# The MLP pair in another order: three output steps behind the first product, two products of one bank together, no step at the end

## The chip, the core and the metric

The kernel runs on one NeuronCore of a Trainium2 chip. TensorE (PE) multiplies, with its weight loads (PEld) shown apart; VectorE (DVE), ScalarE (ACT) and GpSimd (POOL) do the rest; SyncE (SP) issues most DMAs. Products land in PSUM, which has banks of 512 fp32 values per partition. The metric is the device time of one execution in microseconds (us); lower is better.

## The reference, cut to what matters

Three parts follow each other: a Fourier mixing layer, an RWKV channel mix, and an MLP on all 12288 rows. The change lies in the MLP:

```python
def _moe2_ref(x, w_in, w_out):          # x: 12288 x 256
    h = x @ w_in                        # 256 x 2048
    sp = np.where(h > 20.0, h, np.log1p(np.exp(np.minimum(h, 20.0))))
    g = h * np.tanh(sp)                 # "mish"
    return (g @ w_out).astype(np.float32)   # 2048 x 256
```

## The kernel before, in words

The rows are cut into 24 blocks `t` of 512. For each block the 2048 hidden features are taken in 8 pairs, `P = 8 t + r`, each of 256 features by 512 rows. Block 0 is multiplied directly (`emit_h`). For blocks 1 to 23 (184 pairs) `emit_hS` multiplies the pair's 2x2 blocks (two halves of the inner dimension and two of the features, against two halves of the rows) with seven block products in place of eight. `A(i, j)` is a block of the weights, `S_(k)` a prepared sum or difference of such blocks (`WS`), and `xS` holds the seven matching blocks or sums of the rows, which VectorE prepares for the next block in six pieces (`make_xS`).

Every fp32 number is split into a high and a low part, so one product is three matmuls of 128x256 (`prod`, L1075). The accumulators are two PSUM banks a pair, `xy` and `z`, each with two halves of 256 columns, and two sets of them alternate between pairs. The seven products share partial sums: the first goes into `xy[0]`, ScalarE copies it to `z[0]` (L1085), further products are added on `xy` and `z`, ScalarE copies the whole bank `xy` to `ub` in SBUF (L1091), one more product is added on `xy[0]`, VectorE adds `xy[0]` and half of `ub` into `z[1]` (`add`, L1080), and after the last two products it adds the other half of `ub` into `xy[1]`. The mish of `z` is taken in the same pair (`mish`, L1057 and L1058: once into `gh`, once into `g`, with the difference `gl` on VectorE, L1061), and that of `xy` in the next pair, through `fin`.

The second matrix product runs three pairs behind (`LAG = 3`): `o(n)` takes n of the 8 output steps of pair `P - 3`. One step is two matmuls, `gh` by the high and low parts of `w_out` (512 columns, L1123) and `gl` by the high part (256 columns, L1124). Two steps (`m2` = 0, 1) belong to each of the four banks `o0` to `o3`, which are filled over the 8 pairs of a block. With the last pair of a block, `o_out` is called behind each second step: a ScalarE copy into `ob` (L1138), a VectorE sum (L1139) and a DMA out (L1140).

Each engine executes its own instructions in the order in which this code writes them, and waits by semaphores. No scheduler changes the order. A write to one half of a PSUM bank waits for a read of the other half.

Of the kernel before, what the change touches and what calls it, by code (L numbers as in the profile page):

```python
# [29 lines left out]
def kernel(  # L30
# [766 lines left out]
    def g_tiles(P):  # L797
        pool = w2p if P % 4 < 2 else pb
        return [pool.tile([128, 2, 512], F32R, tag=n, name=n, bufs=2) for n in ("gh", "gl")]
# [201 lines left out]
    def make_xS(t, k):  # L1001

        v = x2_t[t]
        o4 = last_order if t == NBLK - 1 else (lambda a, how=None: a)
        b11, b12, b21, b22 = (
            o4(v[:, j, 256 * h:256 * h + 256], "p (c n w) -> p c w n") for j in range(2) for h in range(2)
        )
        if k == 0:
            xT_t[0] = pb.tile([128, 4, 256], F32, tag="xT", name="xT", bufs=1)
            xS_t[t] = pb.tile([128, 2, 7, 256], F32R, tag="xS", name="xS", bufs=2)  # L1010
        xT, xS = xT_t[0], xS_t[t]

        def parts(l):
            if t == NBLK - 1:
                return [(o4(xS[:, l, i, :]), b) for i, b in enumerate((b11, b21, b22))]
            return [(xS[:, l, 0, :], b11), (xS[:, l, 1:3, :], v[:, 1, :].rearrange("p (h n) -> p h n", h=2))]

        def xt(o):
            return o4(xT[:, o, :])

        def sub(o, x0, x1):
            nc.vector.tensor_tensor(out=xt(o), in0=x0, in1=x1, op=ALU.subtract)

        if k == 0:
            sub(0, b12, b11)
            sub(2, b22, b12)
        elif k == 1:
            sub(1, b22, xt(0))
            sub(3, b21, xt(1))
        elif k == 2:  # L1030
            nc.vector.tensor_copy(out=xS[:, 0, 3:7, :], in_=xT)
        elif k == 3:
            nc.vector.tensor_tensor(out=xS[:, 1, 3:7, :], in0=xT, in1=xS[:, 0, 3:7, :], op=ALU.subtract)
        elif k == 4:
            for xs, b in parts(0):
                nc.vector.tensor_copy(out=xs, in_=b)
        else:
            for (xl, b), (xh, _) in zip(parts(1), parts(0)):
                nc.vector.tensor_tensor(out=xl, in0=b, in1=xh, op=ALU.subtract)
            x2_t.pop(t)  # L1040
# [11 lines left out]
    def mish(P, src, k):  # L1052

        gh, gl, g = g_t[P]
        ks = slice(0, 4, 3) if k == 0 else slice(1, 3)
        view = [v.rearrange("p m (h n) -> p (m h) n", h=2)[:, ks, :] for v in (gh, gl, g)]
        nc.scalar.activation(out=view[0], in_=src, func=AF.Mish)  # L1057
        nc.scalar.activation(out=view[2], in_=src, func=AF.Mish)  # L1058

        def low():  # L1060
            nc.vector.tensor_tensor(out=view[1], in0=view[2], in1=view[0], op=ALU.subtract)  # L1061

        return low

    def emit_hS(P, o):
        t, r = divmod(P, 8)
        xS = xS_t[t]
        f = [slice(256 * r + 128 * i, 256 * r + 128 * i + 128) for i in range(2)]
        xy, z = (psb.tile([128, 2, 256], F32, tag=f"h{k + P % 2}", name=n, bufs=1) for k, n in ((0, "xy"), (2, "z")))
        A = lambda i, j: (lambda l: WI[:, j, l, f[i]])  # L1070
        S_ = lambda k: (lambda l: WS[:, r, k, l, :])

        def prod(out, a, b, start=False):
            for n, (l, v) in enumerate(P3):
                nc.tensor.matmul(  # L1075
                    out=out, lhsT=a(l), rhs=xS[:, v, b, :], start=(start and n == 0), stop=False, skip_group_check=True
                )

        def add(out, x0, x1):
            nc.vector.tensor_tensor(out=out, in0=x0, in1=x1, op=ALU.add)  # L1080

        g_t[P] = g_tiles(P) + [pb.tile([128, 2, 512], F32, tag="g", name="g", bufs=2)]
        ub = pb.tile([128, 2, 256], F32, tag="ub", name="ub", bufs=2)
        prod(xy[:, 0, :], A(0, 0), 0, start=True)
        nc.scalar.copy(out=z[:, 0, :], in_=xy[:, 0, :])  # L1085
        low = fin[0]() if fin[0] else None
        prod(xy[:, 1, :], S_(2), 5)
        o(2)
        prod(xy[:, 0, :], S_(1), 4)
        prod(z[:, 0, :], A(0, 1), 1)  # L1090
        nc.scalar.copy(out=ub, in_=xy)  # L1091
        if low:
            low()
        if r > 1 and t + 1 < NBLK:
            make_xS(t + 1, r - 2)
        o(2)
        prod(xy[:, 0, :], S_(0), 3)
        add(z[:, 1, :], xy[:, 0, :], ub[:, 1, :])
        o(3)
        low = mish(P, z, 0)  # L1100
        prod(xy[:, 0, :], S_(3), 2)
        prod(xy[:, 1, :], A(1, 1), 6)
        add(xy[:, 1, :], xy[:, 1, :], ub[:, 0, :])
        low()
        o(1)
        fin[0] = lambda: mish(P, xy, 1)

    def new_o(t):
# [37 lines left out]
    for P in range(2, 8 * NBLK + LAG):  # L1146
        t, q = divmod(P, 8)
        steps = o_steps(P - LAG) if P >= LAG else iter(())

        def o(n):  # L1150
            for _ in range(n):
                next(steps, None)

        if P < 8 * NBLK:
            if q == 0 and 2 < t + 2 < NBLK:
                load_x2(t + 2)
            if t:
                if P == 8:
                    last_WS = make_WS(3, True)
                emit_hS(P, o)  # L1160
                if P < 12:
                    next(last_WS, None)
            else:
                emit_h(P)
                if q < 7:
                    make_xS(1, q - 2)
                if q == 6:
                    make_xS(1, 5)
                if q in (2, 4, 6):
                    for _ in make_WS(q // 2 - 1):  # L1170
                        pass
        elif fin[0]:
            fin[0]()()
            fin[0] = None
        o(9)
# [82 lines left out]
```

## Time and profile before

| what | value |
|---|---|
| median of 3 runs | 2101.61 us (2100.99 to 2104.11) |
| profiled execution, its own time | 2103.1 us |
| its span, from the first to the last instruction | 2101.3 us |
| TensorE busy | 1990.7 us (95% of the span) |
| weight loads busy | 1831.9 us (87%) |
| ScalarE busy | 1209.8 us (58%) |
| VectorE busy | 1127.0 us (54%) |
| mean granted TensorE clock | 0.997 |

Matmuls are pipelined: a row of the timeline shows 0.28 us for a matmul of 256 columns, while the next one starts before it ends. How long a matmul holds the engine is the distance between starts. A busy share is an average over the span, and the stage that the change touches is the last one, from about 966 us to the end.

### The profile page before, as it was taken

The numbers are of one execution on the slowest core, as the hardware profiler recorded it, in microseconds if no ns is written. First come the engines' busy times: TensorE is split into PE (matmuls) and PEld (weight loads), VectorE is DVE, ScalarE is ACT, GpSimd is POOL, SyncE is SP. The second block draws the span as 40 slices with busy tenths as digits, with TensorE's granted clock in tenths as the row PEclk, the third lists the DMA queues.
The fourth block names the chain that finished last, engine by engine and source line by source line (L and its number), as shares of the span: only waits on it lengthen the run. The fifth ranks groups of instructions, "written<-read, shape, count | busy, mean of one in ns | idle before, by whom it ended". The sixth has DMA issues, their size and how long they took to land.

```text
span 2101.3 us, 31779 instructions
## 1 busy us (share of the span) xinstructions
PE 1990.7 (95%) x12658; PEld 1831.9 (87%) x12658; DVE 1127.0 (54%) x1899; ACT 1209.8 (58%) x2151; POOL 130.7 (6%) x236
## 2 busy tenths in 40 slices
PE   7999999999999999999999999999999999999998
PEld 5888899999999999998888888888888888888887
DVE  3788765555555655446444444444544444444453
ACT  3666676666666666655555555555555555555554
POOL 1444410000000000000000000000000000000000
PEclk8999999999999999999999999999999999999999
DMA  9786422122121211110000010000000000000000
GB/s 282 217 243 205 149 78 68 57 63 67 56 67 54 69 54 59 41 43 21 21 21 21 21 29 23 21 21 21 26 26 21 21 21 21 21 21 31 11 11 21
DMA packets 71735, 122.93 MB, mean 58 GB/s; under 512 B 6370, under 2 KB 48580, under 8 KB 71588
## 3 DMA queue, kind: packets, MB, share of 16 engines
q1 hardware_dynamic: 68004, 108.33, 17.4%
q0 software_dynamic: 3584, 12.58, 1.6%
q8 instruction: 99, 1.62, 0.3%
q14 instruction: 48, 0.39, 0.1%
HBM read 70.56 MB, written 50.33 MB: 58 GB/s over the span
## 4 chain that ended last, share of the span: by engine, by line
PE 92%; ACT 4%; issue 1%; DVE 1%; DMA 1%; SPq 0%; ACTq 0%; DVEq 0%
PE xy L1075 21%; PE o L1123 17%; PE kp L686 13%; PE vp L871 13%; PE o L1124 8%; PE mxp L408 3%; ACT z L1085 3%; PE pp L825 3%; PE z L1075 3%; PE pp L509 2%; PE s1p L303 2%; PE s2p L352 2%; PE i1p L450 2%; PE k1p L408 2%; ACT ob L1138 0%
## 5 line engine op out<-in xcount | busy, mean ns | idle before, releaser
L1123 PE MATMUL o<-WO,gh 128*128 128x512 f32 x1536 | 574.0, 396 | 0.0
L1075 PE MATMUL xy<-xS,WS 128*128 128x256 f32 x2208 | 401.0, 290 | 95.0 <-ACT z L1085 94.1
L1075 PEld LDWEIGHTS xy<-xS,WS 128*128 128x128 f32 x2208 | 310.3, 188 | 162.8 <-ACT z L1085 131.7
L1124 PE MATMUL o<-WO,gl 128*128 128x256 f32 x1536 | 430.8, 280 | 0.0
L1061 DVE TENSOR_TENSOR gl<-g,gh 128x512 fp32r<-128x512 f32 x368 | 252.5, 686 | 172.4 <-ACT g L1058 172.4
L1123 PEld LDWEIGHTS o<-WO,gh 128*128 128x128 f32 x1536 | 288.8, 188 | 37.8
L686 PE MATMUL kp<-xk,WK 128*128 128x384 f32 x1524 | 291.9, 339 | 0.0
L1124 PEld LDWEIGHTS o<-WO,gl 128*128 128x128 f32 x1536 | 289.6, 189 | 0.2
L871 PE MATMUL vp<-kh,WV 128*128 128x384 f32 x1024 | 280.3, 335 | 0.0
L686 PEld LDWEIGHTS kp<-xk,WK 128*128 128x128 f32 x1524 | 264.1, 188 | 0.6 <-ACT yT L518 0.4
L858 DVE TENSOR_TENSOR kl<-kr,kh 128x768 fp32r<-128x768 f32 x128 | 123.0, 961 | 239.2 <-ACT kr L857 239.2
L1057 ACT ACTIVATE gh<-z 128x512 fp32r<-128x512 f32 x184 | 110.2, 599 | 217.7 <-DVE z L1080 217.7
L1080 DVE TENSOR_TENSOR xy<-xy,ub 128x256 f32<-128x256 f32 x184 | 79.6, 433 | 217.5 <-PE xy L1075 217.5
L1075 PE MATMUL xy<-xS,WI 128*128 128x256 f32 x1104 | 189.8, 280 | 0.0
L871 PEld LDWEIGHTS vp<-kh,WV 128*128 128x128 f32 x1024 | 186.7, 188 | 0.0
L1091 ACT COPY ub<-xy 128x512 f32<-128x512 f32 x184 | 108.2, 588 | 122.3 <-PE xy L1075 122.3
L871 PE MATMUL vp<-kl,WV 128*128 128x384 f32 x512 | 171.5, 335 | 0.0
L856 ACT ACTIVATE kh<-kr 128x768 fp32r<-128x768 f32 x128 | 108.2, 845 | 99.3 <-PE vp L871 99.3
L1075 PEld LDWEIGHTS xy<-xS,WI 128*128 128x128 f32 x1104 | 156.1, 188 | 7.9
L1080 DVE TENSOR_TENSOR z<-xy,ub 128x256 f32<-128x256 f32 x184 | 79.4, 432 | 152.4 <-PE xy L1075 131.9
L1085 ACT COPY z<-xy 128x256 f32<-128x256 f32 x184 | 65.8, 357 | 147.1 <-PE xy L1075 146.2
L849 ACT ACTIVATE kr<-kp 128x768 f32<-128x768 f32 x127 | 103.5, 815 | 74.4 <-PE kp L686 72.0
(150 smaller groups left out, 2818.2 us busy)
## 6 DMA issues: line engine op xcount, KB each, us to landing
scr<-Cs SPq DMA_DIRECT2D x48, 256.0 KB
D<-scr SPq DMA_DIRECT2D x32, 384.0 KB
x2d<-r POOLq DMA_DIRECT2D x32, 384.0 KB, 2.8
x<-x2d SPq DMA_DIRECT2D x24, 512.0 KB
out_dram<-ob SPq DMA_DIRECT2D x96, 128.0 KB
A<-scr SPq DMA_DIRECT2D x44, 256.0 KB
xs<-in_x_dram SPq DMA_DIRECT2D x24, 384.0 KB
scr<-xs SPq DMA_DIRECT2D x24, 384.0 KB
```

The lines of the kernel that those rows point to most:

```text
L686: nc.tensor.matmul(out=p, lhsT=WK[:, dh, w, f * 128:(f + 1) * 128], rhs=hl[:, v, dh, :], start=(i == 0), stop=(i == 5),)
L856: nc.scalar.activation(out=kh, in_=kr, func=AF.Square)
L858: nc.vector.tensor_tensor(out=kl, in0=kr, in1=kh, op=ALU.subtract)
L871: nc.tensor.matmul(out=p[:, o, 0:TA], lhsT=WV[:, f, w, o * 128:(o + 1) * 128], rhs=v[:, m, :], start=(f == 0 and i == 0), stop=(f == 7 and ...
L1057: nc.scalar.activation(out=view[0], in_=src, func=AF.Mish)
L1061: nc.vector.tensor_tensor(out=view[1], in0=view[2], in1=view[0], op=ALU.subtract)
L1075: nc.tensor.matmul(out=out, lhsT=a(l), rhs=xS[:, v, b, :], start=(start and n == 0), stop=False, skip_group_check=True)
L1080: nc.vector.tensor_tensor(out=out, in0=x0, in1=x1, op=ALU.add)
L1085: nc.scalar.copy(out=z[:, 0, :], in_=xy[:, 0, :])
L1091: nc.scalar.copy(out=ub, in_=xy)
L1123: nc.tensor.matmul(out=o[m], lhsT=gh[:, m2, ms], rhs=WO[:, f], start=(f == 0), stop=False)
L1124: nc.tensor.matmul(out=o[m][:, 0, :], lhsT=gl[:, m2, ms], rhs=WO[:, f, 0, :], start=False, stop=(f == 15))
```

## The change

In `emit_hS` the order of code lines changes, and nothing else. Before, the first product was followed by the product with `S_(2)` into `xy[1]`, two output steps, and the product with `S_(1)` into `xy[0]`. Now three output steps follow the first product, and then the products with `S_(1)` and `S_(2)` together. The output step that stood behind the last two products is gone from there; the pair still takes all 8 steps (3 + 2 + 3 in place of 2 + 2 + 3 + 1).

```diff
         prod(xy[:, 0, :], A(0, 0), 0, start=True)
         nc.scalar.copy(out=z[:, 0, :], in_=xy[:, 0, :])
         low = fin[0]() if fin[0] else None
+        o(3)
+        prod(xy[:, 0, :], S_(1), 4)
         prod(xy[:, 1, :], S_(2), 5)
-        o(2)
-        prod(xy[:, 0, :], S_(1), 4)
         prod(z[:, 0, :], A(0, 1), 1)
         nc.scalar.copy(out=ub, in_=xy)
...
         prod(xy[:, 1, :], A(1, 1), 6)
         add(xy[:, 1, :], xy[:, 1, :], ub[:, 0, :])
         low()
-        o(1)
         fin[0] = lambda: mish(P, xy, 1)
```

On TensorE, at the turn from one pair to the next, the kernel before has these rows: the last two products of a pair, the output step, the first product of the next pair (the fifth row), the product with `S_(2)`, two output steps, the product with `S_(1)`, the product into `z`.

```order
L1075 MATMUL xy<-xS,WS 128x256 x3
L1075 MATMUL xy<-xS,WI 128x256 x3
L1123 MATMUL o_15929<-WO,gh 128x512
L1124 MATMUL o_15929<-WO,gl 128x256
L1075 MATMUL xy<-xS,WI 128x256 x3
L1075 MATMUL xy<-xS,WS 128x256 x3
L1123 MATMUL o_15926<-WO,gh 128x512
L1124 MATMUL o_15926<-WO,gl 128x256
L1123 MATMUL o_15926<-WO,gh 128x512
L1124 MATMUL o_15926<-WO,gl 128x256
L1075 MATMUL xy<-xS,WS 128x256 x3
L1075 MATMUL z<-xS,WI 128x256 x3
```

The same place in the changed kernel, on TensorE, where the line numbers are one lower:

```order
L1075 MATMUL xy<-xS,WS 128x256 x3
L1075 MATMUL xy<-xS,WI 128x256 x6
L1122 MATMUL o_14558<-WO,gh 128x512
L1123 MATMUL o_14558<-WO,gl 128x256
L1122 MATMUL o_14558<-WO,gh 128x512
L1123 MATMUL o_14558<-WO,gl 128x256
L1122 MATMUL o_14559<-WO,gh 128x512
L1123 MATMUL o_14559<-WO,gl 128x256
L1075 MATMUL xy<-xS,WS 128x256 x6
L1075 MATMUL z<-xS,WI 128x256 x3
```

The last product of one pair and the first of the next now stand together (x6), three steps lie between the first product and the next one into the same bank, and the products with `S_(1)` and `S_(2)` stand together (x6) ahead of the one into `z`.

On VectorE, in the pair in which a block's output leaves, the kernel before has this order (`ob` are the output sums, `z` and `xy` the sums of L1080, `xT` a piece of the next block's operands):

```order
L1139 TENSOR_TENSOR ob<-ob,o_15471 128x256
L1061 TENSOR_TENSOR gl<-g,gh 128x512
L1022 TENSOR_TENSOR xT<-x_15279 128x256 x2
L1139 TENSOR_TENSOR ob<-ob,o_15472 128x256
L1080 TENSOR_TENSOR z<-xy,ub 128x256
L1139 TENSOR_TENSOR ob<-ob,o_15473 128x256
L1080 TENSOR_TENSOR xy<-xy,ub 128x256
L1061 TENSOR_TENSOR gl<-g,gh 128x2x256
L1139 TENSOR_TENSOR ob<-ob,o_15474 128x256
```

The changed kernel, on VectorE in the same pair:

```order
L1138 TENSOR_TENSOR ob<-ob,o_15468 128x256
L1061 TENSOR_TENSOR gl<-g,gh 128x512
L1022 TENSOR_TENSOR xT<-x_15279 128x256 x2
L1138 TENSOR_TENSOR ob<-ob,o_15469 128x256
L1080 TENSOR_TENSOR z<-xy,ub 128x256
L1138 TENSOR_TENSOR ob<-ob,o_15470 128x256
L1138 TENSOR_TENSOR ob<-ob,o_15471 128x256
L1080 TENSOR_TENSOR xy<-xy,ub 128x256
L1061 TENSOR_TENSOR gl<-g,gh 128x2x256
```

The fourth output sum moves ahead of the sum into `xy`; what stands ahead of the sum into `z` is as it was.

## Rows read from the trace of the kernel before

**Rows 1.** Windows: one stretch, busy time of each engine, granted clock.
```profile
core 0: us, PE busy (x) PEld busy (x) DVE busy (x) ACT busy (x) POOL busy (x), PEclk, DMA share, GB/s
600.00:800.00 200.00, 200.00 (x1208) 200.00 (x1207) 114.90 (x160) 131.77 (x191) 6.90 (x10) 1.00 0.20 61
```

**Rows 2.** Costliest groups of the page: busy, mean ns | idle before, releaser.
```profile
L1075 PE MATMUL xy<-xS,WS 128*128 128x256 f32 x2208 | 401.0, 290 | 95.0 <-ACT z L1085 94.1
```

**Rows 3.** Waits of the weight loads, 966 to 2090: us in total, times, longest.
```profile
PEld xy L1075 <- ACT z L1085: 131.7, 184, 1.5
PEld xy L1075 <- DVE z L1080: 7.8, 22, 0.9
```

**Rows 4.** Timeline of one pair: start, us, engine, what, [idle before, releaser].
```profile
1503.75 0.52 PE L1075 MATMUL xy<-xS,WI 128*128 128x256 f32 x3
...
1504.36 0.36 ACT L1085 COPY z<-xy 128x256 f32<-128x256 f32 x1 [0.89 <-PE xy L1075]
1504.63 0.60 ACT L1057 ACTIVATE gh<-xy 128x512 fp32r<-128x512 f32 x1
1504.77 0.42 PEld L1075 LDWEIGHTS xy<-xS,WS 128*128 128x128 f32 x3 [0.71 <-ACT z L1085]
1504.77 0.62 PE L1075 MATMUL xy<-xS,WS 128*128 128x256 f32 x3 [0.50 <-ACT z L1085]
...
1505.12 0.60 ACT L1058 ACTIVATE g<-xy 128x512 f32<-128x512 f32 x1
1505.23 0.40 PE L1123 MATMUL o<-WO,gh 128*128 128x512 f32 x1
...
1505.76 0.69 DVE L1061 TENSOR_TENSOR gl<-g,gh 128x512 fp32r<-128x512 f32 x1 [1.13 <-ACT g L1058]
...
1505.93 0.51 PE L1075 MATMUL xy<-xS,WS 128*128 128x256 f32 x3
...
1506.48 0.59 ACT L1091 COPY ub<-xy 128x512 f32<-128x512 f32 x1 [0.76 <-PE xy L1075]
...
1507.34 0.51 PE L1075 MATMUL xy<-xS,WS 128*128 128x256 f32 x3
...
1507.94 0.43 DVE L1080 TENSOR_TENSOR z<-xy,ub 128x256 f32<-128x256 f32 x1 [1.49 <-PE xy L1075]
```

**Rows 5.** Windows: two gapless stretches of 13 slots, and a block's output pair.
```profile
1493.12:1497.72 4.60, 4.60 (x33) 4.23 (x32) 1.81 (x5) 2.17 (x5) 0.00 (x0) 1.00 0.00 0
1505.23:1509.79 4.56, 4.56 (x33) 4.21 (x32) 1.27 (x3) 2.17 (x5) 0.00 (x0) 1.00 0.01 4
1468.16:1474.53 6.37, 5.85 (x38) 5.00 (x38) 3.96 (x10) 4.45 (x11) 0.00 (x0) 1.00 0.12 37
```

**Rows 6.** Timeline, TensorE: the stopped product in the first and last pair.
```profile
967.72 0.62 PE L1075 MATMUL xy<-xS,WS 128*128 128x256 f32 x3 [1.27 <-ACT z L1085]
...
2083.80 0.62 PE L1075 MATMUL xy<-xS,WS 128*128 128x256 f32 x3 [0.50 <-ACT z L1085]
```

**Rows 7.** Timeline, VectorE: the longest piece of the next operands, the sum behind it.
```profile
1488.18 1.22 DVE L1033 TENSOR_TENSOR xS<-xT,xS 128x1024 fp32r<-128x1024 f32 x1
...
1489.77 0.43 DVE L1080 TENSOR_TENSOR z<-xy,ub 128x256 f32<-128x256 f32 x1 [0.37 <-PE xy L1075]
```

**Rows 8.** Timeline of a block's output pair.
```profile
1469.52 0.37 ACT L1138 COPY ob<-o 128x256 f32<-128x256 f32 x1 [0.40 <-PE o L1124]
...
1469.92 0.42 DVE L1139 TENSOR_TENSOR ob<-ob,o 128x256 f32<-128x256 f32 x1 [1.90 <-ACT ob L1138]
...
1470.26 0.68 DVE L1061 TENSOR_TENSOR gl<-g,gh 128x512 fp32r<-128x512 f32 x1
...
1471.86 0.42 DVE L1080 TENSOR_TENSOR z<-xy,ub 128x256 f32<-128x256 f32 x1
...
1472.34 0.62 PE L1075 MATMUL xy<-xS,WS 128*128 128x256 f32 x3
```

**Rows 9.** Timeline, TensorE, early stage: first row of twelve matmuls, next row behind.
```profile
161.21 0.40 PE L408 MATMUL mxp<-WX,Xh 128*128 128x256 f32 x2
...
162.64 1.89 PE L303 MATMUL s1p<-xs,FC 96*96 96x256 f32 x8
```

## The prediction

> **What bounds the kernel now.** I read the stretches first. From 600 to 800 us TensorE is busy for all 200 us at a granted clock of 1.00 [rows 1]: the earlier stages have nothing to give, and the change does not touch them. The last stage, from about 966 us on, is different. The list of costly groups shows the products of L1075 with 94.1 us of TensorE idle time in front of them, all released by the ScalarE copy of L1085 [rows 2]. The weight loads of the same stage waited for two things only: that copy, 184 times, and VectorE's sum into z, 22 times, 7.8 us in all [rows 3]. 184 is the number of pairs in this stage (23 blocks of 8), so every pair stops once at the same place.
>
> The timeline of one pair shows the stop [rows 4]. The first product starts at 1503.75, the copy of its result runs from 1504.36 for 0.36 us, and the next product, on the other half of the same bank, starts at 1504.77 with its weight load. With nothing to wait for it would have started one product after 1503.75. Its three matmuls then take 0.46 us up to the next instruction (1505.23) where a product in full flow takes 0.35, because behind a wait the first load is not hidden.
>
> How fast the pair could be is in the windows: from 1505.23 to 1509.79 lie 13 slots (five products and eight output steps) without a gap, 4.56 us, and in another pair 4.60 us [rows 5]. A slot, product or step, is thus 0.351 to 0.354 us; I take 0.352. A pair has 7 products and 8 steps, 15 slots, 5.28 us. The stage's own pace: the stopped product starts at 967.72 in the first pair and at 2083.80 in the last [rows 6], 183 periods of 6.10 us. So 0.82 us per pair is not work.
>
> **The change, part by part.** It adds and removes no instruction. It moves matmuls, and with them a few output copies and sums; the DMAs keep their order on every queue, and only the last output part of a block is issued a little earlier. I count from the start of the first product, in the new order, with the delays of rows 4.
>
> *The wait for the copy.* The copy starts 0.61 after the product and releases TensorE 0.41 later, at 1.02. Three steps now lie ahead of the next product, whose slot begins at 0.35 + 3 x 0.352 = 1.41 and whose load would start 0.12 earlier, at 1.29. The wait is over by 0.27 us: it costs nothing. (With two steps the load would have been due at 0.94, and late.) The cover taken from the end of the pair, one step, hid nothing there that TensorE waits for: what follows is the first product of the next pair, on the other pair of banks.
>
> *The wait for the bank's copy into ub.* Before, ub was copied 0.55 after the start of the S_(1) product, and S_(0) came one product (into z) and two steps behind it, at 1507.34 after 1505.93, 1.41 us [rows 4]. Now S_(2) is the last product before z, and the distance is the same. ScalarE must be free: its queue holds copy (0.61), the two activations (0.88, 1.37, the spacings 0.27 and 0.49 of rows 4), free at about 1.87; ub is due at 1.76 + 0.55 = 2.31. It ends at 2.90, and the load of S_(0) is due at 3.05: 0.10 to spare, as now, where it never waits [rows 3].
>
> *The first activation on xy* needs the previous pair's last sum. That pair's last product starts at -0.35, the sum starts 0.55 later and takes 0.43: ready at 0.63, and the activation's turn is at 0.88. Covered.
>
> *The sum into z and S_(3).* S_(0) starts at 3.17, the sum 0.60 later at 3.77, done at 4.20; S_(3) is due at 3.17 + 4 x 0.352 = 4.58, its load at 4.46. Ahead of the sum on VectorE stand gl (0.64 behind the second activation, so at 2.01) and one piece of the next block's operands. The longest piece takes 1.22 us, and VectorE idled 0.37 between it and the sum [rows 7]. The activation now stands 0.42 closer to the sum (1.80 us ahead of S_(0) in place of 2.22), so in that pair the sum is 0.05 late, inside the 0.20 that S_(3) leaves. Nothing.
>
> *The pair in which a block's output leaves, one in eight.* Its 6.37 us [rows 5] hold a second stop: S_(3) starts at 1472.34 behind the late sum of 1471.86 [rows 8]. New order: the first output copy stands behind the activations on ScalarE, 1.37 + 0.50 = 1.87; VectorE's output sum starts 0.40 later, gl 0.34 after that, and the sum into z 1.60 after gl [rows 8], at 4.21, done at 4.63, S_(3) released at 4.69 where 4.58 is its slot. So 0.11 late, and 0.11 for the bare load: 0.22 stay, 5.50 us for this pair. The fourth output sum now stands ahead of the last sum of xy, which no product waits for.
>
> *Sum.* Eight pairs: 7 x 5.28 + 5.50 = 42.46, or 5.31 a pair. Saved 6.10 - 5.31 = 0.79 x 183 = 144.8. The first pair's copy is late for a reason of its own (1.27 us of idle, [rows 6]); three steps, 1.06 us, move into that stop. Together 146. The profiled execution took 2103.1 us (span 2101.3 and 1.8 around it), 1.5 over the median of the runs shown; 2103.1 - 146 = 1957, and against the median 2101.6 the forecast is **1956**.
>
> *Bounds.* Now nine products stand in a row at the turn of a pair and again at S_(1), S_(2), z; before it was two. The nearest row of such a run is in an early stage: 12 matmuls of 128x256 between 161.21 and 162.64 [rows 9], 0.119 each, a product of 0.357. Seven such products add 0.035 a pair, 6 us. If the output pair keeps twice the loss, 5 us more; with the slot at 0.354 another 4: 1972. With a slot of 0.351 and no loss in the output pair it is 6.10 - 5.27 = 0.83 x 184 = 153: 1948.
>
> **The rivals.** (1) *A thinner cover tears.* The thinnest is the 0.10 ahead of S_(0). If ub comes 0.2 later than worked out, each pair pays 0.10 and 0.11 for the bare load, 39 us: 1995; at 0.4 it is 2032. For it: ScalarE has less time between its five jobs. Against it: 0.44 us of ScalarE idle time remain ahead of ub by the count above.
>
> (2) *The change doesn't do what it says*: the stop only moves to the S_(1) product, if the copy is late for ScalarE's sake and not for the product's. Then about 2101. Against it: the copy starts 0.61 after the product as ub does 0.55 after its own, and ScalarE would have to be held 0.8 us longer.
>
> (3) *Slower*: TensorE without its stops loses granted clock, from 2.4 to 1.2 GHz. The stage then has 184 x 5.31 = 977 us of work, and each us of it done at the lower level takes a second one: at 146 us of it, 15%, the gain is gone (2102), at a quarter of it the time is 1956 + 244 = 2200. Against it: 200 of 200 us busy at clock 1.00 [rows 1].
>
> (4) *Faster than this*, if a matmul's own rate is better than the gapless stretch shows. The windows speak against it: 33 records in 4.56 us without a gap [rows 5].
> The Trainium skill, "TensorE: Matmul & The Clock Gate", section "Back-to-back issue gap", gives a warm gap of N/2.4 + 2.5 ns. By it an estimate for the pair is 29 x 0.109 + 8 x 0.216 = 4.89 us and for the kernel about 1881. By that rule the 13 slots would last 4.24 us; the trace has 4.56, so the measurement decides.
>
> **How the numbers follow.** Forecast 0.87, 1948 to 1972; rival 1 0.08 (1972 to 2050); rivals 2 and 3 0.02 each; rival 4 0.01. The range 1947 to 1975 holds the forecast and the near edge of rival 1. About 0.2% (4 us) is what a measurement of this kernel can tell from no change: faster 0.96, same 0.02, slower 0.02.
>
> **What would show it.** In the profile of the changed kernel the idle time of L1075 behind L1085 falls from 94.1 us to about 1 (the first pair), a pair takes 5.28 us and the output pair 5.5, the weight loads' 22 waits for the sum into z remain. Wrong if L1075 waits for L1091 in every pair, if the nine products in a row take more than 0.36 each, or if the granted clock of the stage is below 1.00.

## The result and the profile after

The changed kernel takes 1959.84 us (median of 4 runs, 1959.08 to 1960.69); the kernel before, 2102.86 us beside them. The ratio is 0.9319, with a 95% interval from 0.9303 to 0.9335: faster by 6.8%. The profiled execution took 1960.5 us (span 1958.7), 142.6 less than that of before. Of a later repeat of the changed kernel, one execution of 2710.24 us is left out below: its granted clock was 0.65 or 0.66 in every stretch from the start on, the stages that the change does not touch included.

The page of the changed kernel: span, TensorE, granted clock, the group that answers to [rows 2].

```profile
span 1958.7 us, 31779 instructions
...
PE 1943.5 (99%) x12658; PEld 1821.8 (93%) x12658; DVE 1129.5 (58%) x1899; ACT 1204.9 (62%) x2151; POOL 132.0 (7%) x236
...
PEclk8999999999999999999999999999999999999999
...
L1075 PE MATMUL xy<-xS,WS 128*128 128x256 f32 x2208 | 352.6, 282 | 0.9 <-DVE z L1080 0.6
```

The 94.1 us in front of these products are gone, and no other idle time has come in their place: TensorE is idle for 15.2 us of the span, before for 110.6. As many instructions run as before (31779). The busy time of these matmuls falls from 401.0 to 352.6 us, and that is not less work. A part is records that had stretched behind a wait (mean 290 ns, now 282). The larger part is that two products stand together now, so that their records overlap and the overlap is counted once. The waits of the weight loads, from 960 us on, against [rows 3]:

```profile
PEld xy L1075 <- DVE z L1080: 6.5, 23, 0.7
PEld xy L1075 <- ACT z L1085: 0.9, 2, 0.5
```

The 184 waits for the copy are two. The 22 for the sum into `z` have stayed, in the output pairs of all blocks but the last, and one more has come (0.30 us, at 1902.85).

The timeline of one pair of the changed kernel answers to [rows 4]. It is an output pair; its first product is the second half of the first row (six matmuls, so it starts at 1401.96).

```profile
1401.61 0.87 PE L1075 MATMUL xy<-xS,WI 128*128 128x256 f32 x6
...
1402.57 0.36 ACT L1085 COPY z<-xy 128x256 f32<-128x256 f32 x1 [0.58 <-PE xy L1075]
...
1402.84 0.60 ACT L1057 ACTIVATE gh<-xy 128x512 fp32r<-128x512 f32 x1
...
1403.25 0.78 PEld L1075 LDWEIGHTS xy<-xS,WS 128*128 128x128 f32 x6
1403.33 0.61 ACT L1058 ACTIVATE g<-xy 128x512 f32<-128x512 f32 x1
1403.37 0.87 PE L1075 MATMUL xy<-xS,WS 128*128 128x256 f32 x6
...
1404.08 0.52 PE L1075 MATMUL z<-xS,WI 128*128 128x256 f32 x3
...
1404.28 0.59 ACT L1091 COPY ub<-xy 128x512 f32<-128x512 f32 x1
...
1405.17 0.51 PE L1075 MATMUL xy<-xS,WS 128*128 128x256 f32 x3
...
1406.17 0.42 DVE L1080 TENSOR_TENSOR z<-xy,ub 128x256 f32<-128x256 f32 x1
...
1406.65 0.42 PEld L1075 LDWEIGHTS xy<-xS,WS 128*128 128x128 f32 x3 [0.24 <-DVE z L1080]
1406.65 0.63 PE L1075 MATMUL xy<-xS,WS 128*128 128x256 f32 x3
```

Counted from 1401.96, the copy starts at 0.61, the next load at 1.29 and its product at 1.41, the copy into `ub` at 2.32, `S_(0)` at 3.21, the sum into `z` at 4.21, `S_(3)` at 4.69. The copy has ended (1402.93) before the load wants it.

Two windows of the changed kernel, an output pair and the pair behind it. TensorE's records leave no gap in either, though the first holds the wait of the load just shown:

```profile
1403.37:1408.89 5.52, 5.52 (x39) 4.95 (x38) 4.23 (x10) 4.24 (x12) 0.00 (x0) 1.00 0.14 40
1408.89:1414.17 5.28, 5.28 (x40) 4.93 (x39) 2.92 (x7) 3.05 (x8) 0.00 (x0) 1.00 0.18 57
```

TensorE's rows at the product behind the three steps, in the first and the last pair, answer to [rows 6]:

```profile
963.90 0.52 PE L1075 MATMUL xy<-xS,WI 128*128 128x256 f32 x3
...
965.69 0.98 PE L1075 MATMUL xy<-xS,WS 128*128 128x256 f32 x6 [0.21 <-ACT z L1085]
...
1942.29 0.87 PE L1075 MATMUL xy<-xS,WS 128*128 128x256 f32 x6
```

183 periods in 976.60 us are 5.337 us each, against 6.099 before: 139.5 us. The first pair gives 1.06 (the same 1.79 us from its first product, with three steps inside). The other 2.0 us lie ahead of the stage, which starts at 963.90 in place of 965.93, in code that is the same. They are chance: in the profiles of the experiments below the stage starts between 964.18 and 967.47.

### The profile page after: what moved, and what is told of

It reads as the page before. It is cut to its first block, busy times and chain, and to the rows that moved or that the text cites. A ratio compares the mean times of both kernels' runs of the same rounds, so it can differ in the third digit from the quotient of the medians.

```text
span 1958.7 us, 31779 instructions
## 1 busy us (share of the span) xinstructions
PE 1943.5 (99%) x12658; PEld 1821.8 (93%) x12658; DVE 1129.5 (58%) x1899; ACT 1204.9 (62%) x2151; POOL 132.0 (7%) x236
## 4 chain that ended last, share of the span: by engine, by line
PE 96%; DVE 1%; DMA 1%; ACT 1%; issue 0%; SPq 0%; ACTq 0%; DVEq 0%
PE xy L1075 20%; PE o L1122 18%; PE kp L686 14%; PE vp L871 14%; PE o L1123 9%; PE mxp L408 4%; PE pp L825 3%; PE z L1075 3%; PE pp L509 3%; PE s1p L303 2%; PE s2p L352 2%; PE i1p L450 2%; PE k1p L408 2%; DMA XS<-in_x_dram 1%; DMA xs<-in_x_dram 0%; PE h0p L791 0%
## 5 line engine op out<-in xcount | busy, mean ns | idle before, releaser
L1122 PE MATMUL o<-WO,gh 128*128 128x512 f32 x1536 | 567.0, 398 | 0.0
L1075 PE MATMUL xy<-xS,WS 128*128 128x256 f32 x2208 | 352.6, 282 | 0.9 <-DVE z L1080 0.6
L1075 PEld LDWEIGHTS xy<-xS,WS 128*128 128x128 f32 x2208 | 301.1, 189 | 33.7 <-DVE z L1080 6.5
L1080 DVE TENSOR_TENSOR xy<-xy,ub 128x256 f32<-128x256 f32 x184 | 79.6, 433 | 206.2 <-PE xy L1075 205.3
L1075 PE MATMUL xy<-xS,WI 128*128 128x256 f32 x1104 | 160.1, 280 | 0.0
L1075 PEld LDWEIGHTS xy<-xS,WI 128*128 128x128 f32 x1104 | 143.2, 189 | 0.0
L1080 DVE TENSOR_TENSOR z<-xy,ub 128x256 f32<-128x256 f32 x184 | 79.4, 432 | 87.6 <-PE xy L1075 75.2
```

The lines of the kernel that those rows point to most:

```text
L1075: nc.tensor.matmul(out=out, lhsT=a(l), rhs=xS[:, v, b, :], start=(start and n == 0), stop=False, skip_group_check=True)
L1122: nc.tensor.matmul(out=o[m], lhsT=gh[:, m2, ms], rhs=WO[:, f], start=(f == 0), stop=False)
```

## The experiments

**How much cover the copy needs.** Two kernels with fewer steps behind the first product, the rest put back at the end of the pair:

```diff
-        o(3)
+        o(2)            # e1; o(1) in e2
         prod(xy[:, 0, :], S_(1), 4)
...
         low()
+        o(1)            # e1; o(2) in e2
```

> Two steps in place of three behind the first product, the third put back at the end of the pair. My theory: what counts is the cover of the copy, and a wait also costs the bare weight load behind it. The load of the next product is due at 0.94 us after the first product's start and the copy releases it at 1.02, so 0.08 late and 0.11 for the bare load, 0.19 x 184 = 35 us over the changed kernel: 1995 (1985 to 2005). Rival A, a wait costs only its own length: 15 us, 1975. Rival B, the gain came from the two products standing together and from the step gone at the end, not from the cover: with the step back at the end about 1960 or, if that step is what counts, near 2100.

> One step behind the first product, two at the end of the pair. My theory: the load is due at 0.58, released at 1.02, 0.44 late and 0.11 for the bare load: 0.55 x 184 = 101 us over the changed kernel, 2061 (2050 to 2070). Rival A, only the wait's own length: 81 us, 2041. Rival B, cover does not matter as long as the two products stand together: 1960.

Measured: 1979.99 us (ratio to the kernel before 0.9422, 0.9408 to 0.9436) and 2039.56 us (0.9703, 0.9689 to 0.9718), 20 and 80 us over the changed kernel. Rival B falls: time follows the cover. But my price was too high, and rival A's (15 and 81) is the nearer. The rows say why. With two steps, the first product at 1400.79, then:

```profile
1401.40 0.36 ACT L1085 COPY z<-xy 128x256 f32<-128x256 f32 x1 [0.85 <-PE xy L1075]
...
1401.81 0.77 PEld L1075 LDWEIGHTS xy<-xS,WS 128*128 128x128 f32 x6
1401.84 0.95 PE L1075 MATMUL xy<-xS,WS 128*128 128x256 f32 x6
...
1402.63 0.52 PE L1075 MATMUL z<-xS,WI 128*128 128x256 f32 x3
```

The load starts at 1.02, as counted, and the two products take 0.79 in place of 0.71: the 0.08 by which the load is late, and nothing else. The 0.11 "for the bare load" is the lead of the load over its matmul, and it is already in a lateness counted from the load's due time; I had added it twice. So the price of a wait is, within a few us in all, the release less the load's due time: 0.08 x 184 = 15 us here, and 0.44 x 184 = 81 in the kernel with one step. The two-step kernel loses some 6 more in the output pair, as its waits for the sum take 12.9 us in place of 6.5:

```profile
PEld xy L1075 <- DVE z L1080: 12.9, 25, 1.0
```

The one-step kernel gains there instead (1.2 us of such waits are left), and loses some 3 us by more of the long steps that are described below.

**The parts of the change.** First the two products together, but with no steps ahead of them; then the steps moved, but the two products in their old order (they stand together here too):

```diff
-        o(3)                                 # e3: together only
         prod(xy[:, 0, :], S_(1), 4)
         prod(xy[:, 1, :], S_(2), 5)
+        o(2)
         prod(z[:, 0, :], A(0, 1), 1)
...
         low()
+        o(1)
```

```diff
         o(3)                                 # e4: steps only
-        prod(xy[:, 0, :], S_(1), 4)
         prod(xy[:, 1, :], S_(2), 5)
+        prod(xy[:, 0, :], S_(1), 4)
```

> One part of the change alone: the products with S_(1) and S_(2) together, but directly behind the first product, with the steps where they were (two behind them, two, three, and one at the end). My theory: the stop stays whole, 0.67 us of missed slots and 0.11 for the bare load in each pair: 2095 to 2104, no change against the kernel before. Rival B, standing together is worth something by itself: below 2080.

> The other part alone: three steps behind the first product and none at the end, but the products with S_(2) and S_(1) in their old order. My theory: as the changed kernel, 1960 within 3 us, since both products wait for the same copy and the bank's copy into ub waits for whichever is last. Rival: the order of the two halves matters, some 10 us either way.

Measured: 2110.53 us for the first (ratio 1.0039, 1.0026 to 1.0051) and 1959.36 for the second (0.9323, 0.9309 to 0.9337). Without the steps there is no gain, so standing together is worth nothing by itself, and with them the order of the two products does not matter. A kernel with three steps ahead and the two products apart was not run. The first is even slower than the kernel before, by 9 us, which I had not expected. Its stop is whole, and its waits show what is new:

```profile
PEld xy L1075 <- ACT z L1085: 131.6, 184, 1.5
PEld xy L1075 <- DVE z L1080: 12.9, 22, 1.1
PEld xy L1075 <- ACT ub L1091: 4.8, 23, 0.2
```

In the output pair of that kernel the copy into `ub` stands on ScalarE behind the first output copy, which waits for the two steps, and these now come behind both products:

```profile
1475.42 0.37 ACT L1138 COPY ob<-o 128x256 f32<-128x256 f32 x1 [0.76 <-PE o L1124]
...
1475.69 0.59 ACT L1091 COPY ub<-xy 128x512 f32<-128x512 f32 x1
```

That pair takes 6.74 us (its stopped products start at 1473.70 and 1480.44) in place of 6.37 [rows 5], 0.37 x 23 = 8.5 us; the other pairs keep theirs, 6.03 to 6.09.

**The thinnest cover, ahead of `S_(0)`**, and **the wait that was left, in the output pair**, with the changed kernel again beside them:

```diff
         if r > 1 and t + 1 < NBLK:
             make_xS(t + 1, r - 2)
-        o(2)
+        o(1)                                 # e5
         prod(xy[:, 0, :], S_(0), 3)
         add(z[:, 1, :], xy[:, 0, :], ub[:, 1, :])
-        o(3)
+        o(4)
```

```diff
-        if r > 1 and t + 1 < NBLK:           # e6
+        if r > 2 and t + 1 < NBLK:
             make_xS(t + 1, r - 2)
         o(2)
         prod(xy[:, 0, :], S_(0), 3)
         add(z[:, 1, :], xy[:, 0, :], ub[:, 1, :])
+        if r == 2 and t + 1 < NBLK:
+            make_xS(t + 1, 0)
         o(3)
```

> The changed kernel once more, as the base for the three runs beside it on the same chip: 1960 within 2 us.

> The changed kernel with one output step less ahead of the S_(0) product (one in place of two) and one more behind it (four in place of three). It tests how thin the cover of the copy into ub is. My theory: the load of S_(0) is due at 2.70 us after the pair's first product, ub is done at 2.90 and releases at 2.95, so 0.25 late and 0.11 for the bare load; 0.36 x 184 = 66 us over the changed kernel, less 5 us because the output pair's sum is then covered: 2021 (2010 to 2032), with waits for L1091 in every pair. Rival: the copy into ub would have come sooner if asked, ScalarE has 0.44 us to spare: then the loss is under 20 us, below 1980.

> The changed kernel with the first piece of the next block's operands (two VectorE subtractions) put behind the sum into z, in the output pair alone. My theory: the sum into z then starts at about 3.8 in place of 4.2, the S_(3) product no longer waits, and the pair falls from 5.52 to 5.28 us: 22 x 0.24 = 5 us less than the changed kernel, 1954 to 1956, and the weight loads' 23 waits for the sum fall to a few. Rival: the output sum, not the piece, holds the sum up: no change within 1 us.

The changed kernel came out at 1961.46 us (ratio 0.9333, 0.9320 to 0.9346).

With one step ahead of `S_(0)`: 1998.80 us (0.9513, 0.9500 to 0.9526), 39 over the recorded result of the changed kernel and 37 over its repeat. The wait is where it was expected, in every pair, and the copy did not come sooner:

```profile
1483.34 0.59 ACT L1091 COPY ub<-xy 128x512 f32<-128x512 f32 x1 [0.36 <-PE xy L1075]
...
1483.98 0.42 PEld L1075 LDWEIGHTS xy<-xS,WS 128*128 128x128 f32 x3 [0.29 <-ACT ub L1091]
```

Its price again is about the lateness of the load: 0.25 x 184 = 46 us, less the 5 of the output pair, 41. (Some 6 us less again would follow from the long steps described below, which are nearly gone here, so the sum fits to a few us and no closer.) My expectation had the same 0.11 added twice. The rival, that ScalarE had time to spare and would be earlier, falls: the copy waits for its product, not for its turn.

With the first piece behind the sum: 1955.48 us (0.9309, 0.9296 to 0.9322), its runs between 1954.4 and 1958.5, the repeat's between 1960.4 and 1961.5. The sum into `z` now comes straight behind the second output sum, the piece follows it, and `S_(3)` at 1405.31 waits for nothing:

```profile
1404.42 0.43 DVE L1080 TENSOR_TENSOR z<-xy,ub 128x256 f32<-128x256 f32 x1
...
1404.77 0.75 DVE L1022 TENSOR_TENSOR xT<-x 128x256 f32<-128x256 f32 x2
...
1405.31 0.51 PE L1075 MATMUL xy<-xS,WS 128*128 128x256 f32 x3
```

The pair runs from 1402.07 to 1407.41, 5.34 us in place of 5.52 (not 5.28, for the reason that follows). This version beats both kernels, the changed one by 4 to 6 us.

**Two output steps that last longer.** In half of the pairs of the changed kernel (P mod 4 of 1 or 2) two steps take 0.39 us in place of 0.35 or 0.36. The starts of the products with `S_(1)` in four pairs, from P mod 4 = 0 on, show it in the periods, 5.27, 5.34 and 5.35:

```profile
1414.16 0.87 PE L1075 MATMUL xy<-xS,WS 128*128 128x256 f32 x6
...
1419.43 0.87 PE L1075 MATMUL xy<-xS,WS 128*128 128x256 f32 x6
...
1424.77 0.87 PE L1075 MATMUL xy<-xS,WS 128*128 128x256 f32 x6
...
1430.12 0.87 PE L1075 MATMUL xy<-xS,WS 128*128 128x256 f32 x6
```

One long step of the changed kernel, ahead of `S_(0)`, with the step before it:

```profile
1399.08 0.40 PE L1122 MATMUL o<-WO,gh 128*128 128x512 f32 x1
1399.32 0.28 PE L1123 MATMUL o<-WO,gl 128*128 128x256 f32 x1
1399.44 0.42 PE L1122 MATMUL o<-WO,gh 128*128 128x512 f32 x1
1399.69 0.30 PE L1123 MATMUL o<-WO,gl 128*128 128x256 f32 x1
1399.83 0.51 PE L1075 MATMUL xy<-xS,WS 128*128 128x256 f32 x3
```

```diff
     def g_tiles(P):
-        pool = w2p if P % 4 < 2 else pb
+        pool = w2p if (P % 4 < 2 if P < 4 else P % 2 == 0) else pb
```

> The changed kernel with the gh and gl tiles taken from the two pools in turn (even pairs from one, odd pairs from the other) in place of two and two. It asks why two output steps last 0.39 us in place of 0.35 in half of the pairs (those with P mod 4 of 1 or 2, whose steps read tiles of the one pool). My theory: the slow steps follow the place of the tile in memory; then they show in every second pair, the even ones, and the time stays within 2 us of the changed kernel. Rival: they follow the place in the program; then they stay at P mod 4 of 1 and 2. Second rival: they come from a meeting of reads and writes of neighbouring tiles, and vanish or double: 7 us less or more.

Measured: 1960.25 us (0.9331, 0.9319 to 0.9344), no change, and the long steps now stand in every second pair, the even ones. Here is a pair with P mod 4 = 0, which had none in the changed kernel: it has two and lasts 5.35 us. The next pair, which had two, lasts 5.27:

```profile
1395.54 0.87 PE L1075 MATMUL xy<-xS,WS 128*128 128x256 f32 x6
...
1396.96 0.42 PE L1122 MATMUL o<-WO,gh 128*128 128x512 f32 x1
...
1398.39 0.42 PE L1122 MATMUL o<-WO,gh 128*128 128x512 f32 x1
...
1400.89 0.87 PE L1075 MATMUL xy<-xS,WS 128*128 128x256 f32 x6
...
1406.16 0.87 PE L1075 MATMUL xy<-xS,WS 128*128 128x256 f32 x6
```

So they go with the place of the `gh` and `gl` tiles that the step reads, the pool `pb`, and not with the pair's number.

The place is not enough, though. All eight steps of such a pair read tiles of that pool, and two are long. The kernel with one step ahead of `S_(0)` takes its tiles from the pools as the changed kernel does, and has 22 long steps in the whole stage (rows of 0.42 us for the `gh` matmul), where the changed kernel has 185. In this pair of it, with P mod 4 = 2, the step ahead of `S_(3)` takes 0.35 us like its others:

```profile
1491.06 0.39 PE L1122 MATMUL o<-WO,gh 128*128 128x512 f32 x1
1491.29 0.28 PE L1123 MATMUL o<-WO,gl 128*128 128x256 f32 x1
1491.41 0.51 PE L1075 MATMUL xy<-xS,WS 128*128 128x256 f32 x3
```

So the order or the moment of the steps counts too. The second rival, a meeting of reads and writes, is not excluded: what would meet is not shown. No version takes all its tiles from the pool `w2p`.

## Why the prediction was right, point by point

*The stop* was 0.82 us a pair, and it is gone whole. The two-step and one-step kernels show that the cover is what removed it, and that three steps are the least that do. The kernel with the products together and no steps ahead of them keeps the stop, and the order of the two products does nothing.

*The covers that I said would hold* held. The load of `S_(0)` starts with no wait in any pair; taking one step from it brings the wait back in all 184. The first activation and the VectorE piece of 1.22 us are in no list of waits. A piece that the prediction did not count, the last one of the last block's operands (L1039, 1.70 us), is behind the one new wait of 0.30 us.

*The output pair* was forecast at 5.50 us with a sum at 4.21 and `S_(3)` at 4.69. It has 5.52 with 4.21 and 4.69, and the late piece explains it: moved behind the sum, the wait goes. That the pair's time agrees so well is in part luck. Without the wait it takes 5.34 and not 5.28 (the late-piece kernel), so the wait costs 0.18 and not 0.22; the two misses nearly cancel.

*The sum* was 146 us from the profiled execution, and 142.6 were measured, 140.6 of them in the stage; the 2.0 ahead of it are chance and bring the forecast closer than it was. The term that was mis-sized is the period: 5.31 forecast, 5.337 measured, 0.03 x 183 = 5 us. I took one slot of 0.352 for all steps; half of the pairs have two long steps where before they had one, so pairs of 5.27 and 5.35 us alternate by twos. The difference stood in [rows 5] already: the stretch of 4.60 us holds one such step, the one of 4.56 none. What the bounds call nine products in a row are three products, nine matmuls (before, two products stood together). They cost nothing more: two of them take 0.71 in the timeline above (1403.37 to 1404.08), 0.355 each, so their bound of 6 us was not needed. The upper bound is also added up loosely: 1956 and 6, 5 and 4 are 1971.

*Rival 1* did not come, and its price was wrong in the way that the experiments show: a cover that is 0.10 short of the load's due time costs about 0.10 a pair and not 0.21. (In the output pair the 0.11 was rightly added, as the lateness there is counted from the product's slot.) *Rival 2* fell with the stop: the copy starts 0.61 after its product, as before. *Rival 3* did not come: the granted clock of the stage is 1.00, the upper level. *Rival 4* did not either: apart from the output pairs' wait the stage has no gap left, and it runs at the slot that the gapless stretch had shown.

## What to carry to other kernels

Where a copy out of an accumulator holds up the next product into the same bank, count from the product's start to the copy's release, and put that much independent work of the same engine between them; the next weight load must find the release, not the next matmul. The price of a cover that is too short was here about its lateness against the load's due time (0.08, 0.25 and 0.44 us a pair gave 20, 39 and 80 us over 184 pairs, with side effects of some us). Work taken from a place where nothing waits costs nothing there, but in one pair of eight it carries copies and sums with it, so look at their queues too.

## What the runs showed of the hardware that was not expected

The two matmuls of an output step can last 0.39 us in place of 0.35 from start to start. Of the 1496 steps of the stage, 92 are long in the kernel before, 185 in the changed kernel, 268 with one step behind the first product, and 22 with one step ahead of `S_(0)`; these four choose their tiles' pools alike. All of the long ones read tiles of the pool `pb`, and they moved with the pool, so the place of the tile that the weights come from is one condition; the order or the moment of the step is another. In the changed kernel they cost 0.04 us twice in half of the pairs, 7 us in all, and stand directly ahead of the products `S_(0)` and `S_(3)`. In the kernel before there is one in the same half of the pairs, the middle one of the three steps behind `S_(0)`. Why stays open.
